# One decode step of attention with a gated MLP: K loaded one group ahead of V, K of the middle groups in one load of 64 KB rows

## The chip, the core and the metric

The kernel runs on one core of one Trainium2 chip. A core has five engines that run their own instruction streams: TensorE (PE, with its weight loads shown apart as PEld), VectorE (DVE), ScalarE (ACT), GpSimd (POOL) and SyncE (SP). They wait for each other through semaphores. Data comes from the chip's memory (HBM) into the on-chip memory (SBUF) by 16 DMA engines; matmul results stand in PSUM. The metric is the time of one execution on the device in microseconds (us).

## The reference

One token, `x` of shape [1, 1, 512], goes through two branches, and a scalar gate mixes them. All inputs are bf16.

```python
g = sigmoid((x * gate_w).sum(-1, keepdims=True))
# A: attention of 32 query heads over 8 groups of K and V, 32768 keys of 128 each
q = (x @ wq).reshape(1, 1, 32, 128)           # 4 heads share a group's K and V
scores = einsum("bhqd,bhkd->bhqk", q, k) * 128 ** -0.5
o = einsum("bhqk,bhkd->bhqd", softmax(scores), v)
a = o.reshape(1, 1, 4096) @ wo                # wo [4096, 512]
# B: gated MLP
b = (silu(x @ w_gate) * (x @ w_up)) @ w_down  # F = 1792
out = g * a + (1 - g) * b
```

K and V of a group are 8.39 MB each; the eight groups are 134 of the 148 MB that the kernel reads.

## The kernel before

A *page* is 128 partitions of 32 KB in SBUF; there are five. A group's K or V fills two pages: partition p holds 256 consecutive keys, its *halves* b = 0 and 1 of 128 keys each. Pages 0 and 1 (`PG_K`) hold K's two halves, pages 2 and 3 (`PG_V`) hold V, and page 4 (`PG_X`) holds wq at the start and wo at the end. Page 3 also holds w_gate and w_up at the start (`PG_F`).

**The transfers.** SP issues every load, in program order, and each waits on SP until its page is free: wq, x, gate_w, w_gate and w_up, then for each group K half 0, K half 1 and V, then w_down and wo in five pieces. A K half is one load of 128 rows of 32 KB. It waits until `sem_fill` says that the same half of the group before has been transposed (`load_k`, L263). V is one load of 128 rows of 64 KB, for the last group two of 32 KB. It waits until `sem_v_free` says that the V before has been multiplied (`load_v`, L274 and L280). For group 0 V waits for `sem_pe_h`, the end of the products with w_gate and w_up. POOL answers V's one semaphore by raising the second half's too.

**The work on a group**, in a hardware loop over groups on each engine:

1. PE transposes K, taken as fp32 pairs, in units of eight 128 x 128 blocks into one of two PSUM tiles (`emit_fill`, L309); there are eight units to a half, sixteen to a group. DVE copies each unit into SBUF (`ktT`, L635). Two units behind, PE multiplies the copied unit with the queries into `ps_sc` (`emit_scores`, L321). At each half this pipe is filled and drained anew.
2. DVE takes the maximum of each half's scores (L640) and of both (L642). PE transposes it (L343), DVE reduces it (L650) and forms a diagonal (L654), and PE spreads it to all partitions (L347, `emit_max`).
3. ACT scales it into the bias `nbias` (L516) and forms the eight exponentials, with their sums (L523). The profile shows an ACT_TABLE_LOAD in each turn, at L516.
4. PE multiplies the exponentials with V into `ps_o` (`emit_v`, L362): the first half from the fourth exponential on, the second after the eighth.
5. PE adds up the sums (L374), ACT copies `ps_o` (L532), and PE folds it (L383, `emit_reduce`). DVE stores the group's column of `oTw` (L668).

After the loop PE multiplies w_down and the wo pieces as they land, DVE writes the row out and SP stores it. In PE's program the code for this end stands ahead of the start and of the loop: an outer loop of two turns runs the start first.

Of the kernel before, what the change touches and what calls it, by code (L numbers as in the profile page):

```python
# [5 lines left out]
ACT = mybir.ActivationFunctionType  # L6
ALU = mybir.AluOpType
# [5 lines left out]
def bass_gated_mix__gqa_block_cached__swiglu_ffn__decode_kernel(  # L13
# [55 lines left out]
    PG_K = (0, 1)  # L69
    PG_V = 2  # L70
    PG_F = 3
    PG_X = 4
    NPG = 5

    with ExitStack() as es:
# [4 lines left out]
        sem_v = [S_(f"s_v{b}") for b in range(NB)]  # L80
# [81 lines left out]
        esum = T("esum", [128, NB, HPG], FP32)  # L162
        esum2 = T("esum2", [128, HPG], FP32)
# [3 lines left out]
        oTw = T("oTw", [128, (G + 1) * STEP], FP32)  # L167
# [8 lines left out]
        ps_sc = [P(f"ps_sc{i}", [128, 512], FP32) for i in range(NB)]  # L176
# [28 lines left out]

        vpage = page[:, PG_V : PG_V + NB, :].rearrange("p b (r d) -> p b r d", d=DH)
        wq_v = page[:, PG_X, 0 : KC * H * DH].rearrange("p (c n) -> p c n", c=KC)
# [40 lines left out]
        with nc.Block("main") as block:  # L248
            @block.gpsimd
            def _(pool):  # L250
                pool.memset(ones_f[:, :], 1.0).then_inc(sem_ones, 1)
                pool.memset(ones_bf[:, :], 1.0).then_inc(sem_ones, 1)
                for g in range(G - 1):
                    pool.wait_ge(sem_v[0], 16 * (g + 1))
                    pool.sem_inc(sem_v[1], 16)

            @block.sync
            def _(sp):
                def load_k(g, b):
                    if g:  # L260
                        sp.wait_ge(sem_fill, UPG * (g - 1) + UPP * (b + 1))
                    src = A_k_cache[0, g, :, :].rearrange("(p b r) d -> p b r d", b=NB, r=R)
                    sp.dma_start(  # L263
                        page[:, PG_K[b], :].rearrange("p (r d) -> p r d", d=DH), src[:, b, :, :]
                    ).then_inc(sem_k[b], 16)

                def load_v(g):
                    if g:
                        sp.wait_ge(sem_v_free, STEP * g)
                    else:  # L270
                        sp.wait_ge(sem_pe_h, 1)
                    src = A_v_cache[0, g, :, :].rearrange("(p b r) d -> p b r d", b=NB, r=R)
                    if g < G - 1:
                        sp.dma_start(  # L274
                            vpage.rearrange("p b r d -> p (b r d)"),
                            src.rearrange("p b r d -> p (b r d)"),
                        ).then_inc(sem_v[0], 16)
                    else:
                        for b in range(NB):
                            sp.dma_start(vpage[:, b, :, :], src[:, b, :, :]).then_inc(  # L280
                                sem_v[b], 16
                            )
# [8 lines left out]
                for g in range(G):  # L291
                    for b in range(NB):
                        load_k(g, b)
                    load_v(g)
                sp.dma_start(  # L295
                    wd[:, :, :], B_w_down.rearrange("(p j) n -> p j n", j=FC)
                ).then_inc(sem_ld_wd, 16)
                src = A_wo.rearrange("(p j) n -> p j n", j=WOJ)
# [5 lines left out]
            def _(pe):  # L304
                def emit_fill(b, u):
                    kv = page[:, PG_K[b], :].bitcast(FP32)
                    for k in range(RPU):
                        n = u * RPU + k
                        ins = pe.transpose(  # L309
                            pst[u % NST][:, k * 128 : (k + 1) * 128],  # L310
                            kv[:, n * 128 : (n + 1) * 128],
                            ident_f[:, :],
                        )
                    ins.then_inc(sem_fill, 1)
# [15 lines left out]
                def emit_k(i, b):  # L330
                    pe.wait_ge(sem_k[b], i + 16)
                    for u in range(UPP + LAG):
                        if u >= LAG:
                            pe.wait_ge(sem_cp, i + (UPP * b + u - LAG + 1))
                        if u < UPP:
                            emit_fill(b, u)
                        if u >= LAG:
                            ins = emit_scores(b, u - LAG)
                    ins.then_inc(sem_sc, UPP)
# [15 lines left out]
                def emit_v(i):  # L355
                    for b in range(NB):
                        pe.wait_ge(sem_v[b], i + 16)
                        pe.wait_ge(sem_exp, i + UPP * (b + 1))
                        for k in range(R // RQ):
# [5 lines left out]
                                vpage[:, b, k * RQ : (k + 1) * RQ, :],  # L365
# [6 lines left out]
                def emit_reduce(i):  # L372
# [8 lines left out]
                    pe.wait_ge(sem_acc, i + STEP)  # L381
# [10 lines left out]
                def emit_start():  # L392
# [84 lines left out]
                    pe.wait_ge(sem_ps0, 1)  # L477

                    with pe.Fori(0, G * STEP, STEP) as i:
                        for b in range(NB):  # L480
                            emit_k(i, b)
                        emit_max(i)
                        emit_v(i)
                        emit_reduce(i)

                def emit_end():
                    pe.wait_ge(sem_dve_tT, 1)
# [18 lines left out]
            def _(act):  # L506
# [6 lines left out]

                with act.Fori(0, G * STEP, STEP) as i:
                    act.wait_ge(sem_b, i + STEP)
                    act.activation(  # L516
                        nbias[:, :], ps_m[:, M_B0 : M_B0 + HPG], ACT.Copy, scale=-SCALE
                    ).then_inc(sem_nbias, STEP)
                    act.wait_ge(sem_nbias, i + STEP)
                    for b in range(NB):  # L520
                        sc = ps_sc[b][:, :].rearrange("p (t h) -> p h t", h=HPG)
                        for h in range(HPG):
                            act.activation(  # L523
                                ET[:, b * R : (b + 1) * R, h],
                                sc[:, h, :],
# [5 lines left out]
                    act.wait_ge(sem_v_free, i + STEP)  # L531
                    act.activation(part, ps_o[:, :], ACT.Copy).then_inc(sem_acc, STEP)  # L532

            @block.vector
            def _(dve):
# [95 lines left out]
                with dve.Fori(0, G * STEP, STEP) as i:  # L631
                    for b in range(NB):
                        for u in range(UPP):
                            dve.wait_ge(sem_fill, i + (UPP * b + u + 1))
                            dve.tensor_copy(  # L635
                                ktT[:, u % NKT, :], pst[u % NST][:, :].bitcast(BF16)
                            ).then_inc(sem_cp, 1)
                        dve.wait_ge(sem_sc, i + UPP * (b + 1))
# [17 lines left out]
                    ).then_inc(sem_dg, STEP)  # L656
                    dve.wait_ge(sem_exp, i + STEP)
# [9 lines left out]
                    dve.wait_ge(sem_red, i + STEP)  # L667
                    dve.tensor_scalar(  # L668
                        oTw[:, bass.ds(i, HPG)],
                        ps_m[:, M_P0 : M_P0 + HPG],  # L670
                        1.0,
                        None,
                        op0=ALU.mult,
                    ).then_inc(sem_rc, STEP)

                dve.wait_ge(sem_rc, G * STEP)
# [3 lines left out]
                    oTw[:, 0 : G * STEP].rearrange("p (g x) -> p g x", x=STEP)[:, :, 0:HPG],  # L680
# [53 lines left out]
```

## Time and profile before

| | us |
|---|---|
| median of 3 runs (351.57 to 351.81) | 351.74 |
| the profiled execution | 351.67 |
| its span, first to last instruction | 350.4 |
| PE busy | 254.6 (73%) |
| PEld busy | 209.2 (60%) |
| DVE busy | 192.1 (55%) |
| ACT busy | 42.9 (12%) |
| DMA, the data queue's share of 16 engines | 98.4% |
| HBM read, mean over the span | 423 GB/s |

Busy is the time in which an engine executes, and the span is what the profile covers; the execution's own time is 1.3 us longer. The page splits the span into 40 slices and gives the busy share of each engine and of the DMA engines in tenths. Other views of the same execution answer for chosen stretches: the busy time by stretch, the waits by engine, the chain that ended last (followed back from the last instruction), and each load's issue with its time to landing. The trace also holds a record of every DMA packet; here a packet is one row of a load.

### The profile page before, as it was taken

What the parts mean: (1) busy time and instruction counts of PE and PEld (TensorE: products, weight loads), DVE (VectorE), ACT (ScalarE), POOL (GpSimd) and SP (SyncE); (2) the same over time, 40 slices, a digit from 0 to 9 for tenths busy, and PEclk for the clock granted to TensorE, in tenths of its full rate; (3) what the DMA queues carried; (4) which work ended last, traced back from release to release, by engine and by line L of the source; (5) the groups of instructions that cost most, each with busy time, mean ns of one, the idle gap of its engine ahead of it and who ended that gap; (6) DMA issues with size and microseconds to landing.
All of it is one profiled execution on the core that took longest, in us unless ns stands there. A gap on an engine that the chain in (4) does not pass through costs nothing.

```text
span 350.4 us, 8660 instructions
## 1 busy us (share of the span) xinstructions
PE 254.6 (73%) x3871; PEld 209.2 (60%) x3871; DVE 192.1 (55%) x242; ACT 42.9 (12%) x156; POOL 0.4 (0%) x6
## 2 busy tenths in 40 slices
PE   1443986688857994898858993798768893798574
PEld 1113985288725984398726991498627891498431
DVE  4243986068803885068804892088705891198500
ACT  1000000400050002300050005000050005000130
POOL 0000000000000000000000000000000000000000
PEclk9965999699968997689969997889859995899878
DMA  8999999999989999999999999999999999999995
GB/s 337 408 451 419 477 443 384 423 430 456 464 385 417 456 426 430 423 464 434 434 404 419 464 449 400 423 449 434 434 419 419 464 434 415 423 426 434 420 423 205
DMA packets 4914, 148.21 MB, mean 423 GB/s; under 512 B 554, under 2 KB 556, under 8 KB 940
## 3 DMA queue, kind: packets, MB, share of 16 engines
q1 hardware_dynamic: 4908, 148.12, 98.4%
q8 instruction: 5, 0.08, 0.1%
q14 instruction: 1, 0.01, 0.0%
HBM read 148.11 MB, written 0.00 MB: 423 GB/s over the span
## 4 chain that ended last, share of the span: by engine, by line
DMA 69%; PE 25%; DVE 3%; SPq 1%; ACT 1%; issue 1%; DVEq 0%; ACTq 0%
DMA page<-in_A_k_cache_dram 56%; PE pst L309 18%; DMA page<-in_A_wo_dram 12%; PE ps_sc L321 5%; DVE ktT L635 2%; PE ps_o L362 2%; SPq L301 0%; ACT ET L523 0%; ACT L516 0%; SPq L288 0%; SPq L280 0%; DVE pmaxf L640 0%; PE ps_m L347 0%; SPq L295 0%; PE ps_sc L225 0%
## 5 line engine op out<-in xcount | busy, mean ns | idle before, releaser
L635 DVE COPY ktT<-pst 128x2048 bf16<-128x2048 bf16 x128 | 155.4, 1223 | 31.1 <-PE pst L309 23.4
L309 PE MATMUL pst<-ident_f,page 128*128 128x128 f32 x1024 | 140.5, 286 | 15.6 <-DMA page<-in_A_k_cache_dram 10.3
L309 PEld LDWEIGHTS pst<-ident_f,page 128*128 128x128 f32 x1024 | 115.9, 146 | 19.8 <-DMA page<-in_A_k_cache_dram 11.0
L321 PE MATMUL ps_sc<-qcur,ktT 128*128 128x8 bf16 x2048 | 67.8, 166 | 8.6 <-DVE ktT L635 8.6
L321 PEld LDWEIGHTS ps_sc<-qcur,ktT 128*128 128x128 bf16 x2048 | 66.7, 97 | 11.2 <-DVE ktT L635 10.0
L362 PE MATMUL ps_o<-page,ET 128*16 128x512 bf16 x512 | 43.6, 515 | 27.1 <-ACT ET L523 27.1
L362 PEld LDWEIGHTS ps_o<-page,ET 128*16 128x16 bf16 x512 | 15.8, 113 | 51.5 <-issue 36.4
L516 ACT ACT_TABLE_LOAD x8 | 10.3, 1283 | 239.0 <-PE ps_m L347 239.0
L658 DVE TENSOR_TENSOR esum<-esum 128x4 f32<-128x4 f32 x8 | 1.3, 164 | 42.7 <-ACT ET L523 42.7
L523 ACT ACTIVATE ET<-ps_sc,nbias 128x128 bf16<-128x128 f32 x64 | 23.9, 562 | 0.7
L662 DVE RECIPROCAL rS<-ps_sc 128x4 f32<-128x4 f32 x8 | 1.5, 182 | 34.2 <-PE ps_sc L374 34.2
L523 ACT ACTIVATION_READ_ACCUMULATOR ET<-ps_sc,nbias 128x1 f32 x64 | 18.6, 290 | 0.0
L640 DVE TENSOR_REDUCE pmaxf<-ps_sc 128x4 f32<-128x512 f32 x16 | 11.1, 692 | 10.4 <-PE ps_sc L321 10.4
L383 PE MATMUL ps_m<-sel,acc 128*128 128x4 f32 x64 | 8.4, 255 | 3.6 <-ACT acc L532 3.6
L383 PEld LDWEIGHTS ps_m<-sel,acc 128*128 128x128 f32 x64 | 7.7, 191 | 4.3 <-ACT acc L532 4.3
L343 PE MATMUL ps_m<-ident_f,pmax 128*4 128x128 f32 x8 | 2.5, 308 | 9.1 <-DVE pmax L642 9.1
L532 ACT ACTIVATE acc<-ps_o 128x512 f32<-128x512 f32 x8 | 4.8, 597 | 34.5 <-PE ps_o L362 34.5
L347 PE MATMUL ps_m<-diag,ones_f 4*128 4x4 f32 x16 | 3.6, 294 | 6.3 <-DVE diag L654 6.3
L347 PEld LDWEIGHTS ps_m<-diag,ones_f 4*128 4x128 f32 x16 | 3.2, 244 | 8.1 <-issue 8.1
L404 PE MATMUL ps_m<-ones_bf,x_row 1*128 1x1 bf16 x4 | 0.3, 172 | 9.3 <-DMA x_row<-in_A_x_dram 9.3
L343 PEld LDWEIGHTS ps_m<-ident_f,pmax 128*4 128x4 f32 x8 | 0.6, 81 | 9.6 <-issue 9.6
L404 PEld LDWEIGHTS ps_m<-ones_bf,x_row 1*128 1x128 bf16 x4 | 0.2, 114 | 9.6 <-DMA x_row<-in_A_x_dram 9.6
(68 smaller groups left out, 53.8 us busy)
## 6 DMA issues: line engine op xcount, KB each, us to landing
page<-in_A_k_cache_dram SPq DMA_DIRECT2D x16, 4096.0 KB, 27.4
page<-in_A_v_cache_dram SPq DMA_DIRECT2D x2, 4096.0 KB, 27.3
page<-in_A_wq_dram SPq DMA_DIRECT2D x1, 4096.0 KB, 12.3
page<-in_A_wo_dram SPq DMA_DIRECT2D x1, 2048.0 KB, 40.2
page<-in_B_w_gate_dram SPq DMA_DIRECT2D x1, 1792.0 KB, 15.5
page<-in_B_w_up_dram SPq DMA_DIRECT2D x1, 1792.0 KB, 19.4
wd<-in_B_w_down_dram SPq DMA_DIRECT2D x1, 1792.0 KB, 35.8
page<-in_A_wo_dram SPq DMA_DIRECT2D x1, 1024.0 KB, 42.3
```

The costliest lines, as they stand in the source:

```text
L309: ins = pe.transpose(pst[u % NST][:, k * 128 : (k + 1) * 128], kv[:, n * 128 : (n + 1) * 128], ident_f[:, :],)
L321: ins = pe.matmul(ps_sc[b][:, col : col + 2 * HPG], kt[:, k, e, :], qcur[:, e, :], start=(e == 0), stop=(e == 1),)
L343: pe.transpose(ps_m[0:HPG, M_A0 : M_A0 + 128], pmax[:, :], ident_f[:, :]).then_inc(sem_t, STEP)
L347: pe.matmul(ps_m[:, M_B0 : M_B0 + HPG], ones_f[0:HPG, :], diag[:, :], start=True, stop=True,).then_inc(sem_b, STEP)
L362: ins = pe.matmul(ps_o[32 * c : 32 * c + RQ * HPG, :], ET[:, n : n + RQ, :].rearrange("p n h -> p (n h)"), vpage[:, b, k * RQ : (k + 1) * ...
L383: ins = pe.matmul(ps_m[:, M_P0 : M_P0 + HPG], acc[:, q, :], sel4[:, q * HPG : (q + 1) * HPG], start=(q == 0), stop=(q == RQ - 1),)
L516: act.activation(nbias[:, :], ps_m[:, M_B0 : M_B0 + HPG], ACT.Copy, scale=-SCALE).then_inc(sem_nbias, STEP)
L523: act.activation(ET[:, b * R : (b + 1) * R, h], sc[:, h, :], ACT.Exp, bias=nbias[:, h : h + 1], scale=SCALE, accum_out=esum[:, b, h : h + ...
L532: act.activation(part, ps_o[:, :], ACT.Copy).then_inc(sem_acc, STEP)
L635: dve.tensor_copy(ktT[:, u % NKT, :], pst[u % NST][:, :].bitcast(BF16)).then_inc(sem_cp, 1)
L640: dve.tensor_reduce(pmaxf[:, b, :], sc, AX.X, ALU.max).then_inc(sem_d, 1)
L662: dve.reciprocal(rS[:, :], ps_s).then_inc(sem_d, 1)
```

## The change

- **Pages.** K has a ring of three pages, `PG_A`, `PG_B`, `PG_C` (0, 1, 2). Even groups lie in B and C, odd groups in A and B. V has pages 3 and 4. wq shares page 3 and w_gate and w_up page 4 at the start; wo takes page 3 at the end.
- **Order of the transfers.** K(0), K(1), V(0), K(2), V(1), and so on to K(7), V(6), V(7), w_down, wo. K(0) and K(1) come in two halves each; K(2) to K(7) come in one load of 128 rows of 64 KB. K(g) waits for the first half of K(g-1) to be transposed, V(g) for V(g-1) to be multiplied. V(7) comes in two halves in pages C and A, which K has left by then, and wo waits for V(6) to be multiplied.
- **Order on PE.** Each group's page B is transposed first. The units of the second half come in pairs, out of A or C by an If/Else on the group's parity; the pipe runs on through the half. V(g-1) is multiplied and folded between the scores and the maximum of g. V(7) is multiplied after the loop. Two small products ahead of the loop raise the semaphores that the first turn looks for.
- **The other engines.** The bias moves from ACT to DVE, an exponential ahead of the loop (`eone`) loads the table, and ACT copies the last `ps_o` before it forms the exponentials. The two score tiles become one PSUM tensor that ACT reads by the parity. POOL raises K's second semaphore instead of V's. DVE stores the folded column of g-1 in turn g.

```diff
-    PG_K = (0, 1)
-    PG_V = 2
-    PG_F = 3
-    PG_X = 4
+    PG_A, PG_B, PG_C = 0, 1, 2
+    PG_V = 3
+    PG_F = 4
+    PG_Q = PG_V
+    PG_X = PG_V
+    PG_L = (PG_C, PG_A)
...
-                for g in range(G - 1):
-                    pool.wait_ge(sem_v[0], 16 * (g + 1))
-                    pool.sem_inc(sem_v[1], 16)
+                for g in range(1, G):
+                    pool.wait_ge(sem_k[1], 16 * g)
+                    if g > 1:
+                        pool.wait_ge(sem_k[0], 16 * (g + 1))
+                    else:
+                        pool.wait_ge(sem_k1, 16)
+                    pool.sem_inc(sem_k[1], 16)
...
-                def load_k(g, b):
-                    if g:
-                        sp.wait_ge(sem_fill, UPG * (g - 1) + UPP * (b + 1))
+                def load_k(g):
+                    lo = PG_A if g % 2 else PG_B
+                    dst = page[:, lo : lo + NB, :].rearrange("p b (r d) -> p b r d", d=DH)
                     src = A_k_cache[0, g, :, :].rearrange("(p b r) d -> p b r d", b=NB, r=R)
-                    sp.dma_start(
-                        page[:, PG_K[b], :].rearrange("p (r d) -> p r d", d=DH), src[:, b, :, :]
-                    ).then_inc(sem_k[b], 16)
+                    if g > 1:
+                        sp.wait_ge(sem_fill, UPG * (g - 1) + UPP + (g == 2))
+                        sp.dma_start(
+                            dst.rearrange("p b r d -> p (b r d)"),
+                            src.rearrange("p b r d -> p (b r d)"),
+                        ).then_inc(sem_k[0], 16)
+                        return
+                    for b in range(NB):
+                        first = lo + b == PG_B
+                        if g and first:
+                            sp.wait_ge(sem_fill, UPP)
+                        sp.dma_start(dst[:, b, :, :], src[:, b, :, :]).then_inc(
+                            sem_k[0] if first else sem_k1 if g else sem_k[1], 16
+                        )
...
                     if g < G - 1:
+                        if g:
+                            sp.wait_ge(sem_v_free, STEP * (g + 1))
+                        else:
+                            sp.wait_ge(sem_pe_h, 1)
...
+                    for b in range(NB):
+                        sp.wait_ge(sem_fill, UPG * (G - 1 + b))
+                        sp.dma_start(vrows(PG_L[b]), src[:, b, :, :]).then_inc(sem_vl[b], 16)
...
-                for g in range(G):
-                    for b in range(NB):
-                        load_k(g, b)
-                    load_v(g)
+                load_k(0)
+                for g in range(1, G):
+                    load_k(g)
+                    load_v(g - 1)
+                load_v(G - 1)
...
+                sp.wait_ge(sem_v_free, STEP * G)
                 src = A_wo.rearrange("(p j) n -> p j n", j=WOJ)
...
+                def emit_k(i):
+                    pe.wait_ge(sem_k[0], i + 16)
+                    for n in range(UPP):
+                        if n >= LAG:
+                            pe.wait_ge(sem_cp, i + (n - LAG + 1))
+                        emit_fill(PG_B, n)
+                        if n >= LAG:
+                            emit_scores(0, n - LAG)
+                    pe.wait_ge(sem_k[1], i + 16)
+                    odd = i & STEP
+                    for n in range(UPP, UPG + LAG, LAG):
+                        if n < UPG:
+                            for pg in (PG_A, PG_C):
+                                with pe.If(odd > 0) if pg == PG_A else pe.Else():
+                                    for m in range(n, n + LAG):
+                                        pe.wait_ge(sem_cp, i + (m - LAG + 1))
+                                        emit_fill(pg, m - UPP)
+                        else:
+                            pe.wait_ge(sem_cp, i + UPG)
+                        for m in range(n - LAG, n):
+                            ins = emit_scores(m // UPP, m % UPP)
+                            if m % UPP == UPP - 1:
+                                ins.then_inc(sem_sc, UPP)
...
                     with pe.Fori(0, G * STEP, STEP) as i:
-                        for b in range(NB):
-                            emit_k(i, b)
+                        emit_k(i)
+                        with pe.If(i > 0):
+                            emit_v(
+                                [[(sem_v, i), (sem_exp, i)], []], (PG_V, PG_V + 1)
+                            )
+                            emit_reduce(i + STEP)
                         emit_max(i)
-                        emit_v(i)
-                        emit_reduce(i)
+                        emit_sum(i)
...
                 with act.Fori(0, G * STEP, STEP) as i:
-                    act.wait_ge(sem_b, i + STEP)
-                    act.activation(
-                        nbias[:, :], ps_m[:, M_B0 : M_B0 + HPG], ACT.Copy, scale=-SCALE
-                    ).then_inc(sem_nbias, STEP)
+                    act.wait_ge(sem_v_free, i + STEP)
+                    act.activation(part, ps_o[:, :], ACT.Copy).then_inc(sem_acc, STEP)
                     act.wait_ge(sem_nbias, i + STEP)
...
-                    act.wait_ge(sem_v_free, i + STEP)
-                    act.activation(part, ps_o[:, :], ACT.Copy).then_inc(sem_acc, STEP)
+                act.wait_ge(sem_v_free, (G + 1) * STEP)
+                act.activation(part, ps_o[:, :], ACT.Copy).then_inc(sem_acc, STEP)
...
+                    dve.wait_ge(sem_b, i + STEP)
+                    dve.tensor_scalar(
+                        nbias[:, :], ps_m[:, M_B0 : M_B0 + HPG], -SCALE, None, op0=ALU.mult
+                    ).then_inc(sem_nbias, STEP)
```

## The prediction

> **What bounds the kernel now.** I read the DMA rows of the page first, because the page gives every compute engine less than three quarters of the span.
>
> ```profile
> DMA  8999999999989999999999999999999999999995
> ...
> DMA packets 4914, 148.21 MB, mean 423 GB/s; under 512 B 554, under 2 KB 556, under 8 KB 940
> ...
> q1 hardware_dynamic: 4908, 148.12, 98.4%
> q8 instruction: 5, 0.08, 0.1%
> ```
>
> The one data queue keeps the 16 DMA engines busy for 98.4% of the span, and only the first and the last two slices fall off. So a change pays only if it makes bytes cheaper or trims an end; it costs as soon as the queue runs dry. Next the busy time by stretch, three stretches of one group each:
>
> ```profile
> 99.90:138.70 38.80, 30.89 (x461) 25.86 (x461) 22.40 (x26) 3.86 (x18) 0.00 (x0) 0.85 1.00 432
> 138.70:177.50 38.80, 31.24 (x461) 26.34 (x461) 22.31 (x26) 5.13 (x20) 0.00 (x0) 0.85 1.00 432
> 177.50:216.30 38.80, 29.05 (x461) 24.47 (x461) 22.31 (x26) 6.13 (x23) 0.00 (x0) 0.90 1.00 432
> ```
>
> Columns: stretch, length, busy time of PE, PEld, DVE, ACT and POOL, clock, DMA share, GB/s. A group is 16.78 MB and takes 38.80 us at a DMA share of 1.00. Then the chain that ended last (start, length, what):
>
> ```profile
> 121.51 27.70 DMA page<-in_A_k_cache_dram
> ...
> 160.53 27.47 DMA page<-in_A_k_cache_dram
> ...
> 198.14 28.67 DMA page<-in_A_k_cache_dram
> ...
> 304.44 43.44 DMA page<-in_A_wo_dram
> 347.88 0.04 issue
> 347.93 0.41 PE ps_sc L225 x8
> 348.34 0.02 issue
> 348.36 0.29 DVE res_row L699
> ```
>
> The K loads land at 149.21, 188.00 and 226.81: 38.8 apart again. The chain names PE pieces between them, but those only say when SP could issue; the load then waited in the queue behind others. The last weights were issued at 304.44 and landed 43.4 later, all of it queue. Last, how near PE is to being the bound (waited for: total, times, longest):
>
> ```profile
> PE pst L309 <- DMA page<-in_A_k_cache_dram: 10.3, 8, 2.9
> PE ps_o L362 <- ACT ET L523: 27.1, 8, 3.4
> ```
>
> PE waits 1.3 us a group for K, so its own group takes 37.5 of the 38.8 us.
>
> **Step 1, the rows.** K(2) to K(7) go from twelve loads of 128 rows of 32 KB to six of 128 rows of 64 KB. Each DMA engine serves 8 of the 128 rows, so per engine 16 short packets become 8 long ones, six times. V already moves in 64 KB rows, so the trace has the price, in three readings. (a) Issue plus time to landing of each load: from V(g-1)'s landing to K(g)'s second landing 19.43, 19.46, 19.41, 19.41, 19.48, 19.38, 19.40, mean 19.42; from there to V(g)'s landing 19.36, 19.37, 19.41, 19.33, 19.39, 19.44, mean 19.38. Six times 0.04 is 0.24 us. (b) The trace's packet records between 115 and 322 us: 1,217.9 ns for 32 KB (1,455 packets), 2,422.6 for 64 KB (640). 2 x 1,217.9 - 2,422.6 = 13.2 ns, times 48 = 0.63 us. (c) Consecutive records overlap by 2.7 ns, so one packet fewer saves 13.2 - 2.7 = 10.5 ns, times 48 = 0.50 us. I take (c), which accounts for the overlap that (b) leaves out and isn't rounded to 0.1 like (a): **0.5 us off**, bounds 0.2 and 0.65.
>
> [...]
>
> **Step 2, the start.** The queue now carries K(0), K(1), V(0) instead of K(0), V(0), K(1): the same bytes. K(1)'s first half has a page of its own and no wait. Its second half waits for eight transposed units of K(0), which today are done at 44.21 (the issue of K(1)), while the queue is full until about 42.5 + 9.7 = 52.2: 8 us early. V(0) is queued behind that wait; its own condition was met at 24.86. Then K(2) waits for nine units of K(1). K(1) lands near 62; today's PE starts V(0) at 63.77, so it will be free about 64, and nine units take about 11.5 us: issue near 76, against a queue filled to 62 + 19.4 = 81.4. **5 us early, the narrowest place.** Cost 0; every us beyond 5 costs one.
>
> **Step 3, the middle.** Call the landing of K(g) L. K(g+1) waits for the first eight units of K(g), 10.1 to 11.4 us in the chain now: issue near L + 11.5, while V(g-1) fills the queue to L + 19.4. V(g) is behind it on SP and waits for V(g-1)'s multiplication: scores some 23.5 us, V 5.4 (the V rows of the timeline run 5.0 to 5.6), so L + 29, against K(g+1) landing at L + 38.7. 8 and 9.7 us early; cost 0.
>
> **Step 4, PE's own group.** No draining at the half: 0.5 off (the first scores of a drain wait 0.54). The reductions L640 (0.69) and L642 lie beside V: 1.1 off. The Exp table load (ten us in eight, 1.28 each) leaves the loop: 1.3 off. But PE no longer has the V product to start after four exponentials (295.62): the next thing on PE, the sum of L374, waits for all eight, which run 293.88 to 296.87, and for L658 (0.16), so about 1.6 on. Four If/Else pairs on PE have no row: from 0 (the loop's own back edge shows no gap beyond the K wait) to 1 us; I take 0.5. Together 0.8 off, 36.7 of 38.7 us, **nothing on the path** while DMA covers it. If that cover went, the excess would first eat the 5 to 8 us above. DVE does the same 16 copies (1.22) and the bias; ACT loses work. POOL's relay of the K semaphore answers a wait that PE reaches 11 us later. SP issues six fewer loads of 0.33 us while it mostly waits (177.2 us at L263): 0.
>
> **Step 5, the end.** Behind K(7) come V(6), two halves of V(7), w_down, wo: that is V(6) more than today behind K(7), and one V less ahead of it, so the last byte's place in the queue is the same. V(7)'s second half waits for all of K(7), about L + 23, with the queue full to L + 29.1; wo waits for V(6) multiplied, L + 29, with the queue full to L + 43. O2 is ready at 342.45 today, 0.5 us ahead of its first weights; tomorrow the last V half (landing about 333) is multiplied at once, not after the exponentials at 334.3, so O2 comes 1 to 2 us earlier. The end stays with the last wo piece: cost 0, and no gain either, since the weights don't land earlier for it.
>
> **Sum.** The profiled execution took 351.67 (span 350.4, 1.3 around it). 351.67 - 0.5 = 351.17. The median of the runs stands 0.07 above that execution, so 351.24: forecast **351.25**, own range 350.9 to 351.6.
>
> **The rivals.** *A, the queue runs dry (slower).* PE reaches K(2)'s ninth unit, or a later group's eighth, too late: from 5 us of delay at K(2) each us is lost once; and if PE's group passes 38.7 us, the delay grows six times. Against: 2 us of room by step 4. For: the branches have no row. At 7 us of delay: 351.25 + 2 = 353.3; with 2 us per group over 38.7, 12 us of delay over 8 of cover, 355.
>
> [...]
>
> *B, code on the slowest DMA engine.* The five 16 KB code packets took 1.02 to 1.07 us, and at the end the 16 engines finish between 345.3 and 347.4, five near 347 (packet records). PE's program grows by 64 transposes and, at the end, a second V. One more page on an engine that is already late moves the last byte by 1.05: 352.3.
>
> *C, the same the other way.* The pages fall on engines that started early; the latest, 0.35 us behind the next ones, loses that lead or a little more: 350.7 (0.55 below the forecast).
>
> *D, the change does not do what its rows are for.* K in 64 KB rows costs what it costs now (reading (a) is near that): 351.74, no change. Against it stand (b) and (c), which are V's rows and not K's.
>
> **How the numbers follow.** What a measurement tells from no change is about 0.2%, 0.7 us: below 351.04 is faster, above 352.44 slower. Forecast 0.60, of which 0.10 lies below 351.04; A 0.11, all slower; B 0.12, of which 0.03 over 352.44; C 0.11, faster; D 0.06. Faster 0.10 + 0.11 = 0.21; slower 0.11 + 0.03 = 0.14; same 0.65. The range 350.6 to 352.6 takes in the forecast, D, B and most of C, and leaves out A and tails, 2 in 10.
>
> **What would show it.** A group's DMA share stays at 1.00 and the K landings come 38.7 apart; the data queue stays at 98% or more; PE's wait for K rises from 10.3 us in total. The table loads in the loop, eight, are gone. Wrong: a stretch with a DMA share of 0.9 or less between 40 and 340 us (A; then see PE before it), code packets after 115 us (A by the branches), or the last landing over 348 with full shares before (B).

## The result, and the profile after

The changed kernel takes 353.74 us (median of 9 runs, 352.18 to 354.68) against 351.59 (9 runs, 351.36 to 352.01): **0.55% slower**, ratio 1.0055, 95% interval 1.0039 to 1.0070. Its runs differ by 2.5 us, those of the kernel before by 0.65. The profiled execution took 353.74, 2.07 more than that of before.

From the page of the changed kernel, the DMA share in 40 slices and the queues:

```profile
DMA  8999999998899999998998998999999989989996
...
q1 hardware_dynamic: 4044, 148.12, 97.9%
q8 instruction: 6, 0.10, 0.1%
```

The same bytes, now 97.9% of a longer span. The two slices from 79 to 97 us are below 9. Some later ones read 8 too, but the slices are 8.8 us long, a packet is counted whole in the slice in which it starts, and packets are now twice as long; stretches of whole groups tell more. The busy time by stretch of the changed kernel (stretch, length, PE, PEld, DVE, ACT, POOL, clock, DMA share, GB/s):

```profile
60.00:78.00 18.00, 11.03 (x122) 10.65 (x123) 8.24 (x13) 3.00 (x16) 0.00 (x0) 0.65 0.97 416
78.00:84.00 6.00, 5.99 (x103) 5.72 (x102) 5.74 (x6) 0.00 (x0) 0.00 (x0) 1.00 0.67 240
84.00:102.00 18.00, 14.64 (x243) 10.72 (x241) 8.87 (x14) 1.14 (x4) 0.00 (x0) 0.91 0.95 411
102.00:140.70 38.70, 31.23 (x461) 26.99 (x461) 22.07 (x27) 4.83 (x28) 0.00 (x0) 0.83 1.00 434
...
219.40:258.10 38.70, 30.47 (x461) 26.00 (x461) 21.97 (x27) 3.59 (x17) 0.00 (x0) 0.85 1.00 434
```

From 102 us on every group has a share of 1.00 at 434 GB/s, where it was 432. The loss is one gap between 78 and 84 us: by the packet records an engine is idle there for 2.6 us on average, and from 84 us to the end of the V loads none is. (The 0.95 of the next stretch comes from packets that start before 84 us.) What SP issued around it (start, length, line, load):

```profile
45.04 0.43 SPq L298 DMA_DIRECT2D page<-in_A_v_cache_dram  x1
81.17 0.33 SPq L278 DMA_DIRECT2D page<-in_A_k_cache_dram  x1
97.94 0.33 SPq L298 DMA_DIRECT2D page<-in_A_v_cache_dram  x1
117.11 0.33 SPq L278 DMA_DIRECT2D page<-in_A_k_cache_dram  x1
```

and, for the same four loads, V(0), K(2), V(1) and K(3), the DMA view's time from issue to landing (the last column):

```profile
page<-in_A_v_cache_dram SPq DMA_DIRECT2D x1, 36.3
...
page<-in_A_k_cache_dram SPq DMA_DIRECT2D x1, 22.1
...
page<-in_A_v_cache_dram SPq DMA_DIRECT2D x1, 24.6
...
page<-in_A_k_cache_dram SPq DMA_DIRECT2D x1, 24.8
```

Issue plus landing gives 81.3, 103.3, 122.5 and 141.9. V(1) and K(3) each land 19.3 after the load before them; K(2) lands 21.9 after V(0), 2.6 us too much. It was issued 0.2 us before the last load in the queue had landed. V(1) and K(3) were issued 5.3 and 5.4 us ahead of that moment. In the kernel before SP issued the second half of K(1), V(1) and the first half of K(2) at

```profile
55.99 0.33 SPq L263 DMA_DIRECT2D page<-in_A_k_cache_dram  x1
69.25 0.33 SPq L274 DMA_DIRECT2D page<-in_A_v_cache_dram  x1
81.73 0.33 SPq L263 DMA_DIRECT2D page<-in_A_k_cache_dram  x1
```

and the first two landed after

```profile
page<-in_A_k_cache_dram SPq DMA_DIRECT2D x1, 4096.0 KB, 25.3
page<-in_A_v_cache_dram SPq DMA_DIRECT2D x1, 31.4
```

The same reckoning gives 12.0 us ahead for V(1) (K(1) landing at 81.29) and 18.9 for K(2) (V(1) landing at 100.65). So K(2) is issued at nearly the same time in both kernels; only what lies in the queue at that time differs.

The chain of the changed kernel, first through the end of its first turn, then late (start, length, what):

```profile
53.95 1.02 issue
...
59.48 0.17 DVE pmax L705
59.65 2.65 issue
62.30 0.39 PE ps_m L381
...
68.46 4.80 PE pst L334 x24
...
192.34 27.04 DMA page<-in_A_k_cache_dram
...
230.70 27.40 DMA page<-in_A_k_cache_dram
...
270.14 26.67 DMA page<-in_A_k_cache_dram
...
328.33 21.60 DMA page<-in_A_wo_dram
...
349.97 0.41 PE ps_sc L234 x7
```

The K loads land at 219.38, 258.10 and 296.81: 38.72 and 38.71 apart, where it was 38.80. Six groups at 0.09 are 0.5 us gained; 2.6 lost at K(2) less 0.5 is 2.1, the 2.07 of the two profiled executions. The end is as before: the last weights land, one group of products, the row. In the first turn PE stands still twice with nothing to wait for: 1.02 us inside a unit of transposes and 2.65 us between the maximum (L705) and its transpose (L381).

PE's wait for K fell, although DMA is later; from the waits of the changed kernel (total, times, longest):

```profile
PE pst L334 <- DMA page<-in_A_k_cache_dram: 6.4, 4, 2.8
```

PE waits in four turns instead of eight: in the others it reaches K late. That is the lag of the first turn being worked off, by some 1.3 us a group at first (K(3) is issued 5.4 us ahead, K(4) 6.7). The prediction had expected this wait to rise above 10.3.

### The profile page after: what moved, and what is told of

It reads as the page before. It is cut to its first block, busy times and chain, and to the rows that moved or that the text cites. A ratio compares the mean times of both kernels' runs of the same rounds, so it can differ in the third digit from the quotient of the medians.

```text
span 352.4 us, 8780 instructions
## 1 busy us (share of the span) xinstructions
PE 263.5 (75%) x3875; PEld 221.1 (63%) x3875; DVE 190.0 (54%) x251; ACT 33.4 (9%) x143; POOL 0.4 (0%) x6
## 3 DMA queue, kind: packets, MB, share of 16 engines
q1 hardware_dynamic: 4044, 148.12, 97.9%
## 4 chain that ended last, share of the span: by engine, by line
DMA 45%; PE 44%; issue 4%; DVE 3%; ACT 2%; SPq 1%; ACTq 0%; DVEq 0%
DMA page<-in_A_k_cache_dram 39%; PE pst L334 30%; PE ps_sc L346 8%; DMA page<-in_A_wo_dram 6%; PE ps_o L401 4%; ACT ET L583 2%; DVE ktT L695 2%; PE ps_m L424 1%; PE ps_sc L413 0%; SPq L326 0%; PE ps_m L385 0%; ACT acc L576 0%; DVE gm L713 0%; SPq L311 0%; ACTq L583 0%
## 5 line engine op out<-in xcount | busy, mean ns | idle before, releaser
L695 DVE COPY ktT<-pst 128x2048 bf16<-128x2048 bf16 x128 | 153.5, 1221 | 34.8 <-PE pst L334 30.5
L334 PE MATMUL pst<-ident_f,page 128*128 128x128 f32 x1024 | 148.8, 301 | 7.6 <-DMA page<-in_A_k_cache_dram 6.4
L334 PEld LDWEIGHTS pst<-ident_f,page 128*128 128x128 f32 x1024 | 127.7, 156 | 11.5 <-DMA page<-in_A_k_cache_dram 6.9
L346 PE MATMUL ps_sc<-qcur,ktT 128*128 128x8 bf16 x2048 | 64.2, 166 | 6.3 <-DVE ktT L695 6.3
L346 PEld LDWEIGHTS ps_sc<-qcur,ktT 128*128 128x128 bf16 x2048 | 63.8, 97 | 8.0 <-DVE ktT L695 7.0
L401 PE MATMUL ps_o<-page,ET 128*16 128x512 bf16 x512 | 41.2, 494 | 0.4 <-issue 0.4
L583 ACT ACTIVATE ET<-ps_sc,nbias 128x128 bf16 x64 | 23.9, 556 | 52.3 <-DVE nbias L721 52.3
L413 PE MATMUL ps_sc<-esum,ones_f 128*128 128x4 f32 x16 | 4.5, 351 | 31.1 <-DVE esum L733 31.1
L713 DVE TENSOR_REDUCE gm<-ps_m 4x1 f32<-4x128 f32 x8 | 2.2, 278 | 43.9 <-PE ps_m L381 43.9
L413 PEld LDWEIGHTS ps_sc<-esum,ones_f 128*128 128x128 f32 x16 | 4.0, 312 | 31.5 <-issue 31.5
L381 PE MATMUL ps_m<-ident_f,pmax 128*4 128x128 f32 x8 | 2.3, 282 | 3.7 <-issue 3.7
## 6 DMA issues: line engine op xcount, KB each, us to landing
wd<-in_B_w_down_dram SPq DMA_DIRECT2D x1, 1792.0 KB, 20.8
```

The lines of the kernel that those rows point to most:

```text
L334: ins = pe.transpose(pst[u % NST][:, k * 128 : (k + 1) * 128], kv[:, n * 128 : (n + 1) * 128], ident_f[:, :],)
L346: ins = pe.matmul(ps_sc[b][:, col : col + 2 * HPG], kt[:, k, e, :], qcur[:, e, :], start=(e == 0), stop=(e == 1),)
L381: pe.transpose(ps_m[0:HPG, M_A0 : M_A0 + 128], pmax[:, :], ident_f[:, :]).then_inc(sem_t, STEP)
L401: ins = pe.matmul(ps_o[32 * c : 32 * c + RQ * HPG, :], ET[:, n : n + RQ, :].rearrange("p n h -> p (n h)"), v[:, k * RQ : (k + 1) * RQ, :], ...
L413: pe.matmul(ps_s, ones_f[:, :], esum2[:, :], start=True, stop=True,).then_inc(sem_s, STEP)
L583: act.activation(ET[:, b * R : (b + 1) * R, h], sc[:, h, bass.ds(bank, R)], ACT.Exp, bias=nbias[:, h : h + 1], scale=SCALE, accum_out=esum ...
```

## The experiments

Theory 1: the queue runs dry at K(2), because the new order leaves little in it, and the longer rows give 0.5 us back. Theory 2: the loss lies in the end. Theory 3: PE's new code costs time by itself. All times of a kernel are medians with the lowest and highest run; a ratio is taken against the kernel before, run beside it, and its interval is the 95% one.

### w_down ahead of K(2)

```diff
+                    if g == 1:
+                        sp.dma_start(
+                            wd[:, :, :], B_w_down.rearrange("(p j) n -> p j n", j=FC)
+                        ).then_inc(sem_ld_wd, 16)
                 load_v(G - 1)
-                sp.dma_start(
-                    wd[:, :, :], B_w_down.rearrange("(p j) n -> p j n", j=FC)
-                ).then_inc(sem_ld_wd, 16)
```

> The load of w_down (1.8 MB, 4.3 us at the queue's rate, a tile of its own) is moved from the end of the queue to just behind V(0), ahead of K(2)'s wait. Theory 1 (the queue runs dry at K(2), 2.5 us of idle DMA near 80 us, and the rows give 0.5 us back): the gap near 80 us is gone, no slice below 0.95 there, the time falls by 2.5 to about 351.1 us, 0.5 below the kernel before, and the spread of its runs (now 352.2 to 354.7) falls below 0.6 us. Theory 2 (the loss lies in the end, where wo waits for V(6) and V(7) for all of K(7)): w_down no longer covers that end, so no gain, or a loss of up to 4 us; about 353.7 or more. Theory 3 (the new code on PE costs time by itself): about 353.7, no change.

Measured: 352.22 (351.13 to 352.81, 11 runs), ratio 1.0012 (1.0003 to 1.0022); the profiled execution took 351.13. Its busy time by stretch:

```profile
78.00:84.00 6.00, 6.00 (x104) 5.72 (x103) 5.73 (x7) 0.00 (x0) 0.00 (x0) 1.00 1.08 453
```

PE is as late as in the changed kernel (K(2) is issued at 81.04), but the gap is gone and with it 2.6 us of the profiled time. Theory 1 holds for the gap, and theory 3 doesn't: PE's program is the same as in the changed kernel, and the time is 351.13. The runs miss the expectation in one point: six of eleven lie between 352.2 and 352.8, so there is a second loss that comes and goes.

### K(2) held back by two more units

```diff
-                        sp.wait_ge(sem_fill, UPG * (g - 1) + UPP + (g == 2))
+                        sp.wait_ge(sem_fill, UPG * (g - 1) + UPP + 3 * (g == 2))
```

> The changed kernel, but K(2) waits for 11 transposed units of K(1) instead of 9, nothing else: K(2) is issued two units (2.6 us) later. Theory 1: the gap near 80 us grows by 2.6 us and the time with it, to about 356.3. Theories 2 and 3: the queue has cover there, no change, about 353.7.

Measured: 357.86 (353.94 to 359.59, 4 runs), ratio 1.0194 (1.0171 to 1.0217): 4.1 us more than the changed kernel (3.4 without the longest run), where 2.6 was expected. In the profiled execution, the fastest of the four, PE began its second turn 2.3 us earlier than in the changed kernel, so K(2) was issued only 0.4 later (81.59), and the time is only 0.2 above. The direction holds in three runs of four, which lie above every run of the changed kernel. The size is not shown: the four runs lie 5.7 us apart, more than the two units are worth.

### The same lateness in the kernel before

```diff
-                        sp.wait_ge(sem_fill, UPG * (g - 1) + UPP * (b + 1))
+                        sp.wait_ge(sem_fill, UPG * (g - 1) + UPP * (b + 1) + 2 * (g == 2 and b == 0))
```

> The kernel before, with K(2)'s first half held back by two more transposed units (2.6 us), as in the late run of the changed kernel. The trace of before has that load 18.5 us ahead of the queue's end. Theory 1: no change, 351.6 within 0.2. If lateness of K(2) on PE's side costs time in itself, whatever the queue holds: up to 2.6 us more, 354.

Measured: 351.63 (351.55 to 351.99, 10 runs), ratio 1.0000 (0.9991 to 1.0009). Two units of lateness cost nothing where the load is 18.9 us ahead.

### K(2) in two halves

```diff
+                    if g == 2:
+                        sp.wait_ge(sem_fill, UPG)
+                        sp.dma_start(dst[:, 1, :, :], src[:, 1, :, :]).then_inc(sem_k2, 16)
+                        sp.wait_ge(sem_fill, UPG + UPP + 1)
+                        sp.dma_start(dst[:, 0, :, :], src[:, 0, :, :]).then_inc(sem_k[0], 16)
+                        return
...
+                    if g == 2:
+                        pool.wait_ge(sem_k2, 16)
```

> K(2) comes in two halves: the one for page C, which K(0) left at about 57 us, is issued then, the one for page B as now after nine units of K(1). The end of the queue stays as in the changed kernel. Theory 1: 9.7 us of cover at the narrow place, so the gap goes as with w_down moved; about 351.2 us. Theory 2: no change, 353.7. Theory 3: no change.

Measured: 352.34 (351.19 to 354.04, 12 runs), ratio 1.0024 (1.0010 to 1.0038); profiled 351.37, no gap near 80 us. With the end unchanged the gap goes all the same, so theory 2 does not explain it. It also shows what a single load of 64 KB rows asks for: two free pages at once, when page C had been free since 56 us and page B was not. But the runs reach 354.0. In the profiled execution V(1) and K(3) are now the narrow places, about 5 us ahead (landing 24.5 and 24.3 us after their issue, less the 19.4 that the load itself takes).

### Both remedies

The two edits above, w_down ahead of K(2) and K(2) in two halves, in one kernel.

> Both remedies at once: w_down behind V(0), and K(2) in two halves with the one for page C issued as soon as that page is free. The two alone left runs up to 352.8 and 354.0 us. Theory 1, refined (the changed order leaves the queue only 5 to 8 us ahead, where the kernel before had 11 to 18; PE's progress varies by several us from run to run, and the slow runs are those in which the queue runs dry at K(2), V(1) or K(3)): now every load up to K(4) is issued at least 8 us ahead, the runs draw together within 0.4 us near 351.1 to 351.2, ratio 0.998 to 0.999. Rival (the extra time of the slow runs is not the queue's cover but something in PE's new code that reaches the end, or the end itself): median stays near 352.2 and the spread above 1 us.

Measured: 351.27 (351.03 to 352.66, 12 runs), ratio 0.9995 (0.9986 to 1.0004). Nine runs lie between 351.0 and 351.6, one at 351.8 and two at 352.4 and 352.7. Better, but not settled. The chain of its profiled execution ends otherwise than before:

```profile
346.26 0.63 PE ps_sc L224 x8
...
346.92 0.61 ACT acc L778
...
347.57 0.64 PE ps_sc L235 x24
```

Here PE is last and no load: with w_down gone from the end, V(7) lands right ahead of wo, and PE's work on V(7) no longer fits beside the transfer of wo. The last weights had landed at 347.48, about as early as in the run with w_down alone (347.42, where VectorE's row began 0.38 later, at 347.80); here the row begins at 348.23, so the end costs about 0.4 us. Theory 2 was wrong of the changed kernel and right of this remedy. The two runs above 352.4 have no profile, and 0.4 us doesn't explain them.

### Short rows at the same issue times

On the kernel with both remedies; POOL's relay also waits for the other half from K(2) on:

```diff
-                        sp.dma_start(
-                            dst.rearrange("p b r d -> p (b r d)"),
-                            src.rearrange("p b r d -> p (b r d)"),
-                        ).then_inc(sem_k[0], 16)
+                        bb = PG_B - lo
+                        sp.dma_start(dst[:, 1 - bb, :, :], src[:, 1 - bb, :, :]).then_inc(sem_k2, 16)
+                        sp.dma_start(dst[:, bb, :, :], src[:, bb, :, :]).then_inc(sem_k[0], 16)
```

> The kernel with both remedies, but K(3) to K(7) come as two loads of 128 rows of 32 KB at the moment at which the one load of 64 KB rows was issued, page B's half last, so that PE starts when it did. Only the length of the rows differs, in five groups. If a 64 KB row saves 10.5 ns against two of 32 KB: 8 x 5 x 10.5 ns = 0.42 us more than the kernel with both remedies, about 351.6. If the rows bring nothing: no difference.

Measured: 351.99 (351.47 to 353.42, 12 runs), ratio 1.0017 (1.0004 to 1.0029). The median is 0.72 above the kernel with both remedies, the fastest run 0.44 above its fastest. The medians can't settle an expected 0.42 with these spreads; the fastest runs agree with it. The traces do settle it: from K(3) to K(7) the landings come 38.80 us apart, where the kernel with both remedies has 38.72, and from K(2)'s landing to K(7)'s it takes 194.02 instead of 193.61 us, 0.41 more, with no idle engine in either.

### Every K in halves, each as soon as its page is free

On the changed kernel, with the same addition to POOL's relay:

```diff
+                        bb = PG_B - lo
+                        sp.wait_ge(sem_fill, UPG * (g - 1))
+                        sp.dma_start(dst[:, 1 - bb, :, :], src[:, 1 - bb, :, :]).then_inc(sem_k2, 16)
                         sp.wait_ge(sem_fill, UPG * (g - 1) + UPP + (g == 2))
-                        sp.dma_start(
-                            dst.rearrange("p b r d -> p (b r d)"),
-                            src.rearrange("p b r d -> p (b r d)"),
-                        ).then_inc(sem_k[0], 16)
+                        sp.dma_start(dst[:, bb, :, :], src[:, bb, :, :]).then_inc(sem_k[0], 16)
```

> The changed kernel with its order and its ring, w_down at the end as there, but every K from K(2) on comes in two halves of 32 KB rows: the one for the page that is free a group earlier is issued at once, the one for page B as now. Theory 1 with the single load as its cause (a load of 64 KB rows needs two free pages at once, and only one is free): about 9.7 us more cover at every K, no dry queue, runs within 0.4 us of each other, and without the saving of the longer rows about 351.6, equal to the kernel before. If the order itself (V a group late) is what costs: still 353 or more.

Measured: 352.25 (351.69 to 354.07, 12 runs), ratio 1.0020 (1.0007 to 1.0033): the expected 351.6 was missed. The single load isn't the only narrow place. V(1), issued at 96.91, took

```profile
page<-in_A_v_cache_dram SPq DMA_DIRECT2D x1, 24.6
```

to land at 121.5. The K half ahead of it, issued at 81.81, took 18.9 and landed at 100.7, so V(1) landed 20.8 after it, 1.4 us too late, though issued 3.8 us ahead. V(1) can't come earlier: there is one V buffer, and V(0) leaves it only when turn 1 has multiplied it. So V a group behind K costs cover of its own.

### The maximum ahead of V

On the changed kernel, PE's products for the maximum of g come ahead of V(g-1) again, and the fold also waits for the bias:

```diff
+                        emit_max(i)
                         with pe.If(i > 0):
                             emit_v(
...
+                            pe.wait_ge(sem_nbias, i + STEP)
                             emit_reduce(i + STEP)
-                        emit_max(i)
```

> [...] In the first turn the skipped V then stands behind the maximum, and the 2.65 us in which PE stood still before the maximum's transpose, if they come from the jump over the V code, run beside the exponentials. Theory 1 with that as the cause of the late K(2): K(2) is issued about 2.5 us earlier, near 78.7 us, the gap shrinks from 2.5 to 0.5 us or less, time about 351.5. If the standstill is not the jump, or comes again elsewhere on the path, the gap stays and the time too, 353.7. Theory 2: no change.

Measured: 354.24 (353.40 to 355.09, 5 runs), ratio 1.0065 (1.0052 to 1.0078), no better. The standstill ahead of the maximum's transpose is gone: PE waits there its ordinary 1.14 us for VectorE's maximum, as in the kernel before. But V is now multiplied after the maximum in every turn, so V(1) is issued at 100.61 instead of 97.94, and the DMA engines stand idle there (packet records: at 101 us) as well as at 80. As a test of the standstill's cause this was too blunt; the next one is not.

### The maximum ahead of the jump in the first turn only

```diff
+                        with pe.If(i < 1):
+                            emit_max(i)
                         with pe.If(i > 0):
                             emit_v(
...
                             emit_reduce(i + STEP)
-                        emit_max(i)
+                            emit_max(i)
```

> The changed kernel with one thing moved on PE, in the first turn alone: there the maximum's two products stand ahead of the jump over the V code, in the other turns behind V as now. If the 2.65 us for which PE stood still ahead of the maximum's transpose in the first turn come from that jump, they now run beside the exponentials (3.9 us on PE's wait for them), K(2) is issued about 2.5 us earlier (near 78.6 instead of 81.2 us), and the gap in the queue, idle and slow restart together 2.7 us, shrinks to 0.5 us or nothing: profiled near 351.5, median 351.5 to 352.3, since PE's progress still differs from run to run. If the standstill has another cause it comes back elsewhere: K(2) near 81, 353.7.

Measured: 352.19 (351.32 to 353.57, 12 runs), ratio 1.0016 (1.0004 to 1.0028), 1.6 us below the changed kernel's median. The chain of its profiled execution, which was one of the longer ones (352.93):

```profile
53.97 2.09 issue
...
61.30 0.17 DVE pmax L707
61.48 0.14 issue
61.61 0.39 PE ps_m L381
```

The 2.65 us between maximum and transpose are 0.14: they did come from the jump over V's code, the first time that PE makes it. The profiles of all the kernels agree. In the seven with the maximum behind that jump, the transpose starts 1.6 us after a 16 KB code packet has ended (60.71 to 62.30 in the changed kernel; 1.59 to 1.62 in all). In the five with the maximum ahead of it, PE waits there only for VectorE (1.14 us in this one). But K(2) was issued at 80.75, not at 78.6: the other standstill took 2.09 here instead of 1.02, and the granted clock fell to 0.50 earlier (from 55.5 to 58.9 us it was 0.50 here and 1.00 in the changed kernel), so that the nine transposes behind that standstill took 2.08 us instead of 1.19.

### Both remedies and the maximum ahead of the jump

The kernel with both remedies and the edit just shown.

> The kernel with both remedies (w_down behind V(0), K(2) in halves) and the maximum ahead of the jump in the first turn. Theory 1: K(2), V(1) and K(3) are issued another 2 to 2.5 us further ahead (V(1) about 10, K(3) about 10 us instead of 7.8 each), so the two slow runs in twelve of that kernel (352.4 and 352.7) don't come: median 351.15 to 351.25, all runs within 0.5 us, ratio 0.9985 to 0.999. If those slow runs are not a dry queue near V(1) and K(3), they come as often as before and the median stays at 351.3.

Measured: 351.57 (351.20 to 352.10, 11 runs), ratio 1.0000 (0.9992 to 1.0009). The runs above 352.2 are gone, but the median rose instead of falling, and the runs lie within 0.9, not 0.5. The end of the profiled execution (351.73) again shows PE last: the last weights landed at 347.44, VectorE's row began at 348.41, about 0.6 us later than the weights alone would have it. In this execution the end is the bound, and the cover gained at V(1) doesn't touch it.

### w_down back at the end, and w_down split

The first keeps K(2) in halves and the maximum ahead of the first jump, with w_down at the end as in the changed kernel. The second does this to it:

```diff
+                    if g == 1:
+                        load_wd(0, FC // 2)
                 load_v(G - 1)
-                sp.dma_start(
-                    wd[:, :, :], B_w_down.rearrange("(p j) n -> p j n", j=FC)
-                ).then_inc(sem_ld_wd, 16)
+                load_wd(FC // 2, FC)
```

> w_down back at the end of the queue; K(2) in two halves and the maximum ahead of the jump in the first turn. It tells the two causes apart that are left for the slow runs with w_down early: a dry queue at V(1) and K(3), or an end in which PE, and no longer the last weights, is last (the profile with both remedies shows that: the last product of the end waits for no load). If the end: all runs within 0.5 us, median 351.15 to 351.3, ratio 0.9985 to 0.999. If V(1) and K(3): slow runs of up to 353 us as with K(2) in halves alone, a little rarer since PE is some 2.5 us earlier, median 351.5 to 352.

> As the one beside it, with half of w_down (0.9 MB, 2.15 us of queue) behind V(0) and half at the end: 2.15 us more cover at V(1) and K(3), 2.15 us less at the end. If V(1) and K(3) make the slow runs, they become fewer and the median falls toward 351.2; if the end makes them, the median rises by up to 0.3 us against the one beside it.

Measured, at the end: 351.30 (351.16 to 352.72, 12 runs), ratio 0.9989 (0.9980 to 0.9998). Split: **351.26 (351.10 to 351.51, 11 runs), ratio 0.9983 (0.9975 to 0.9992)**, faster than both kernels (by 0.2% than the kernel before), and with the smallest spread of all. With w_down at the end the expectation was not met cleanly: the median is the one expected if the end makes the long runs, but a run of 352.72 came all the same. The time of V(1) from issue to landing, first with w_down at the end:

```profile
page<-in_A_v_cache_dram SPq DMA_DIRECT2D x1, 22.8
```

and with w_down split:

```profile
page<-in_A_v_cache_dram SPq DMA_DIRECT2D x1, 26.5
```

The first of these executions was one of the longer ones (351.84): V(1) was issued 2.9 us ahead, the packet records show idle engines at 98 us, and it landed 0.5 us late; K(3), 3.3 us ahead, lost less than 0.1. With w_down split V(1) is 7.1 us ahead, no engine is idle before the end, and the last weights are last again. So each of the two causes is seen in profiles: a nearly dry queue at V(1) with w_down at the end, and an end without cover (0.4 and 0.6 us) with w_down at the front. That the split removes the long runs is likely and not shown: two of twelve against none of eleven can be chance, and the run of 352.72 has no profile.

## Why the prediction was wrong

**Step 1, the rows, was right.** 0.5 us was forecast. K landings 38.71 to 38.72 apart instead of 38.80 give it, and with short rows at the same issue times they were 38.80 apart again. That answers rival D: the rows do what they are for.

**Step 2, the start, failed**, and rival A, which named this place, came true instead. The step put K(2)'s issue at 76 us, 5 us ahead of the queue's end at 81.4, and called the cost zero. The queue's end was right (81.3). The issue came at 81.17. Three terms were mis-sized:

- PE was to be free for K(1) at about 64 and was at 68.46. The two standstills, 1.02 and 2.65, which the step had left out, are the greater part; the second comes from the jump over V's code (shown by the maximum ahead of the jump). The first falls inside a block of transposes and ends 1.5 us after a 16 KB code packet (52.42 to 53.50 in the packet records). The twelve profiles with the new PE program all have it, 0.72 to 2.52 us long; it ends 1.3 to 1.5 us after that packet, whose end lies anywhere between 52.4 and 54.8. That PE waits for code there too is the author's estimate from these times; no experiment took that packet away. Behind the maximum's transpose another 1.4 us were missed: the step let PE be free when V began before, 4.8 us after the transpose (58.98 to 63.77), but it is free only when the sum over all eight exponentials is done, 6.2 us after it (62.30 to 68.46). Step 4 had counted that wait, step 2 had not.
- Nine units were to take 11.5 us and took 12.7 (68.46 to 81.14). For the first 4.2 us of them the granted clock was 0.50; in the kernel before it was 1.00 for all of K(1)'s first half (71.6 to 81.7).
- "Every us beyond 5 costs one" left out what it takes to fill a dry queue. Issued 0.2 us ahead of the end, K(2) cost 2.6 us, not nothing.

What failed is thus the step's time for PE in the first turn, and with it the term "cost 0": the queue ran dry.

**Step 3, the middle**, put the loads 8 and 9.7 us ahead; K(3) and V(1) were 5.4 and 5.3, and the later ones 7 to 10. PE carried the lag of the first turn with it and worked it off slowly. That was enough in the profiled execution. That it is not always enough, the remedies at K(2) show: with that gap closed, runs of 352 to 354 us remained. The two longer executions of this kind that were profiled (353.06 with every K in halves, 351.84 with w_down back at the end) have idle engines at V(1); for the other longer runs of these kernels there is no profile.

**Step 4, PE's group**, was near: turns 1 and 2 took 36.97 and 37.46 us (68.46 to 105.43 to 142.89) against 36.7, and the eight table loads in the loop are gone. **Step 5, the end**, held: 21.6 us of queue behind the last issue.

**Rival A's odds.** It was given 0.11, since step 4 left PE 2 us of room a group. That room says nothing of a first turn. The place had 5 us of cover by a sum of estimates over 80 us, where the kernel before has 12 to 19; so 0.11 was too low for it. The branches were put at 0.5 us a group, since the loop's back edge showed no gap. In the kernel before the last of the five code packets ended at 110.3 us. The changed kernel has six; the last ended at 68.2 us, none came in turns 1 to 7 or at the end, and PE stood still for 2.65 us at the first jump into code not yet passed. Rivals B and C (a page there is a 16 KB code packet) weren't tested.

**Open.** Why PE's progress through the first 80 us differs by several us between runs. The profiles show two things that differ: the length of the first standstill (0.72 to 2.52 us) and the time at which the granted clock falls to a half (55.3 to 59.0 us). What sets either isn't shown. The mean granted clock of a run (0.82 to 0.85 in the nine runs of the changed kernel) doesn't order the times, and there is one profile for each kernel.

## What to carry to other kernels

When a kernel is bound by transfers, count for every load how long before the queue's end it is issued, in the profile before and by the new order, and look at the smallest number; a reordering that keeps every byte can still take the cover away. A cover of 5 us that rests on a sum of estimates is a chance and not a zero, and a first turn (code run for the first time, no earlier work in the queue; here standstills of 1.02 and 2.65 us) has to be counted apart from the steady state. Joining two loads into one saves a little per row (here 0.08 us a group, 38.72 against 38.80) and asks for both destinations at once; splitting only the load at the narrow place, moving part of an unrelated load in front of it, and taking the first turn's standstill off the path kept nearly all of the gain.

## What the runs showed of the hardware

In these runs a queue that was nearly dry cost more than its idle time. In the changed kernel the 16 engines end their last packet of V(0) between 78.83 and 80.85, so the first of them runs out 2.5 us before the landing (81.3) from which the time ahead is counted. K(2) is issued at 81.17, and its first packets start 0.95 us later. An engine is idle for 2.6 us on average, and the first 64 KB packet of nearly every engine takes 2.8 to 3.4 us instead of 2.42, together 0.65 us per engine (packet records). With every K in halves the engines were idle for only 0.26 us on average at V(1), yet their next packets took up to 4.2 us and the load landed 1.4 us late, although it had been issued 3.8 us ahead of the landing before it.

How far ahead a load has to be issued has no sharp edge in these runs. At 2.9 us V(1) lost 0.5 and at 3.3 us K(3) less than 0.1 (w_down back at the end), at 3.8 us V(1) lost 1.4. At 4.5 us or more no load of the profiled executions left an engine idle for more than 0.05 us on average.
